# GpSimd's subtractions and additions issued as two operations of half the columns, in an attention and two-MLP kernel

## The chip, the core and the metric

The kernel runs on one core of a Trainium2 chip. Its engines work side by side, each on an instruction stream of its own: TensorE (PE in the profile; PEld is its weight loads), VectorE (DVE), ScalarE (ACT), GpSimd (POOL) and SyncE (SP), which issues most DMAs. The metric is the device time of the one core in microseconds.

## What is computed

The reference is three blocks, one after the other, on 4 batches of 576 tokens, d_model 512 (8 heads of 64):

```python
scores = scale * np.matmul(q, k.transpose(0, 1, 3, 2))
mask = (rel >= 0) & (rel < 128)
scores = np.where(mask, scores + bias[None], -1000000000.0)     # ALiBi bias, causal window of 128
attn = np.exp(scores - np.max(scores, axis=-1, keepdims=True))
attn = attn / (np.sum(attn, axis=-1, keepdims=True) + 1e-09)
x = heads_joined(np.matmul(attn, v))
# block 1
h = np.maximum(x.transpose(0, 2, 1) @ w_tok1, 0.0) @ w_tok2     # over tokens, 576 -> 256 -> 576
u = x + h.transpose(0, 2, 1)
u = u + np.maximum(u @ w_ch1, 0.0) @ w_ch2                      # over channels, 512 -> 1536 -> 512
# block 2
xn = (u - mean) / np.sqrt(var + 1e-06) * g_ln
out = u + np.maximum(xn @ w_ch1, 0.0) @ w_ch2                   # 512 -> 2048 -> 512
```

## The kernel before

The 2304 tokens are 18 tiles of 128. Every fp32 operand of a matmul is split into a high part and a low part: ScalarE rounds `x` to `hi` (fp32r), then `lo = x - hi` is made by VectorE or GpSimd. A product is then three matmuls (hi by hi, hi by lo, lo by hi), of 128x128 weights and 512 columns as a rule.

Three stages follow each other. **Attention with the token MLP** fills the first 150 us or so: per tile, scores (`ps_s`, L596), softmax on DVE and ACT, transposes (`ps_t`), masks by GpSimd (`pf`, L663), values (`ps_v`), and, a tile at a time, the token MLP (`tok`); GpSimd makes `xl = u - xh` of each tile and the low parts `wt1l`, `fewl` of its weights. **The channel MLP of block 1** and **that of block 2** follow. Each walks over tiles 0 to 7, then 16 and 17, then 8 to 15, and over the hidden features in steps of 256. The groups of eight tiles use a Strassen-like scheme with seven products (`seven_products`, L977): sums and differences of the input quarters (`st`, made by `prep_wide` from transposes `p`) and of the weight halves (`st`, made by `w1_of`, L930). Their low parts are `xl` and `w1l`; `w2l` is the low part of the second weight matrix. The hidden activations are `hh` (ACT) and `hl` (DVE). The second matmul of the MLP (`second`, L1036) writes `acc`, a PSUM tile with two buffers, and DVE adds each `acc` to the residual `u` (L1056); so PE can begin the `acc` after next only when DVE has done that addition.

Weights come as float64 and are decoded: `rh` and `rw` are loaded, ACT makes `e`, DVE makes `s` (L419, L421), `m` (L423) and `y` or `w` (L431). In block 2, `y` is scaled by g_ln (L476).

The order of instructions on every engine is computed while the program is built, by a list scheduler (`Plan.order`, L205). Each operation lists its cost on every engine that may take it; an operation that both DVE and POOL may take goes to POOL unless DVE would finish it sooner by the table (`sooner`, L223; DVE must win by 1200 ns). The costs are `dve(n)` = 150 + n/0.97 and `pool_tt(n)` = 150 + 2.4 n, in ns. The helper `minus` (L372) makes all the subtractions and additions above, and is called through `split` (L377), `split_x`, `w_split`, `x_tile`, `load_f64_split` and directly by `prep_wide` and `w1_of`; in the profile they all stand at line 374, told apart by their tiles. An engine takes its instructions strictly in the order of its stream.

Of the kernel before, what the change touches and what calls it, by code (L numbers as in the profile page):

```python
# [102 lines left out]
class Plan:  # L103
# [186 lines left out]
    def emit(self):  # L290
        for k in self.order():
            self.ops[k][1](self.taken[k])


def dve(n, fast=False):
    return 150 + n / (1.92 if fast else 0.97)
# [6 lines left out]
def pool_tt(n):  # L303
    return 150 + 2.4 * n
# [10 lines left out]
def block_kernel(tc, qT, kT, v, wt1, wt2, wa1, wa2, wb1, wb2, g, bias, out):  # L315
    nc = tc.nc
    NF1, NF2 = FF1 // P, FF2 // P
    pl = Plan()
# [5 lines left out]
    ENGINE = {"DVE": nc.vector, "POOL": nc.gpsimd}  # L324
# [30 lines left out]
    def several(x):  # L355
        return x if isinstance(x, list) else [x]
# [13 lines left out]
        pl.op({e: cost[e] for e in on}, emit, several(src), several(dst))  # L370

    def minus(dst, get, a, ga, b, gb, n, on=("DVE", "POOL"), alu=ALU.subtract, also=()):  # L372
        cost = {"DVE": dve(n), "POOL": pool_tt(n)}
        pl.op({e: cost[e] for e in on}, lambda e: ENGINE[e].tensor_tensor(get(), ga(), gb(), alu),  # L374
              [*several(a), *several(b), *also], several(dst))

    def split(hi, ghi, lo, glo, x, gx, n, on_hi=("ACT", "DVE", "POOL"), on_lo=("DVE", "POOL")):  # L377
        copy(hi, ghi, x, gx, n, on_hi)
        minus(lo, glo, x, gx, hi, lambda: ghi().bitcast(F32), n, on_lo)
# [287 lines left out]
    def normalize(i):  # L667

        rs = rs_t[i]
        ut = buf("atb", [P, H // 2, P], F32, "ut", 2)  # L670
        copy(ut, lambda: ut.t, pv, lambda: pv.t, DM, ("ACT",), True)

        def transposes():
            for p in range(4):
                nc.tensor.transpose(pv.t[:, p], ut.t[:, p], ident.t)

        op({"PE": 400}, transposes, [ut, ident], [pv])
        rc = buf("small", [P, H, 1], F32, "rc", 2)
        op({"POOL": 250}, lambda: nc.gpsimd.tensor_scalar(rc.t, rs.t, 1e-9, None, ALU.add), [rs], [rc])
        op({"DVE": 170}, lambda: nc.vector.reciprocal(rc.t, rc.t), [], [rc])  # L680
        minus(u[i], lambda: u[i].t.rearrange("p (h d) -> p h d", h=H), pv,
              lambda: pv.t.rearrange("p a (b d) -> p (a b) d", b=2), rc, lambda: rc.t.to_broadcast([P, H, D]), DM,
              ("DVE",), ALU.mult)
# [169 lines left out]
    def split_x(x, b, psum):  # L853

        hi, lo = x
        copy(hi, lambda: hi.t, b, lambda: b.t, CW, ("ACT",), psum)
        minus(lo, lambda: lo.t, b, lambda: b.t, hi, lambda: hi.t.bitcast(F32), CW, ("DVE",) if psum else ("DVE", "POOL"))
# [265 lines left out]
    for s in range(len(steps) + 1):  # L1123
# [5 lines left out]
        layer, c, tiles, n = steps[s]  # L1129
# [86 lines left out]
```

## Time and profile before

| | us |
|---|---|
| median of 3 runs | 854.21 (851.65 to 856.25) |
| the profiled execution | 853.47 |
| its span, first to last instruction | 851.8 |
| PE busy in it | 831.5 (98%) |
| DVE busy | 635.6 (75%) |
| ACT busy | 394.5 (46%) |
| POOL busy | 341.3 (40%) |

The profiled execution lies 0.74 us under the median and 1.7 us over its own span. A stretch of time in the profile is read by its busy time per engine, the clock that TensorE was granted (1.00 is its upper level, 2.4 GHz) and the list of waits; "idle 1.32 <-DVE u" behind an instruction says that its engine stood still for 1.32 us before it and that DVE's writing of `u` ended that.

### The profile page before, as it was taken

The page shows a single profiled execution, that of the slowest core. Times are in us where ns is not written, and L with a number is a line of the kernel's source. Part 1 is how long each engine was busy: PE and PEld are TensorE (multiplying, and loading weights), DVE is VectorE, ACT ScalarE, POOL GpSimd, SP SyncE. Part 2 cuts the span into 40 slices and gives each one's busy share as a digit, 9 for nine tenths or more (in the row PEclk, how much of TensorE's full clock was granted, in tenths as well). Part 3 has the DMA queues.
Part 4 walks back from the last instruction along what each step waited for, and adds up shares of the span by engine and source line. Part 5 has one row for each costly group of instructions (what it writes and reads, how often), then busy time and mean ns, then how long its engine had stood idle before and what let it go on. Part 6 is the DMA issues. An engine that isn't in the chain of part 4 may idle for free.

```text
span 851.8 us, 13204 instructions
## 1 busy us (share of the span) xinstructions
PE 831.5 (98%) x4478; PEld 687.5 (81%) x4478; DVE 635.6 (75%) x1308; ACT 394.5 (46%) x952; POOL 341.3 (40%) x356
## 2 busy tenths in 40 slices
PE   7999999989999999999998999999999999999998
PEld 6777878768888887788887888788889888888886
DVE  5787778987887989987888856988667755555554
ACT  6788776553434535234367322336358322222221
POOL 2675445554433656522236524614234712221110
PEclk9999999999999999999999999999999999999999
DMA  8678726467666799977752521777477762221112
GB/s 296 188 213 258 246 101 202 157 188 256 223 216 230 242 324 326 358 249 267 257 201 74 171 92 48 262 265 251 172 247 238 251 203 75 75 74 50 50 50 99
DMA packets 73698, 164.96 MB, mean 194 GB/s; under 512 B 8352, under 2 KB 8480, under 8 KB 73632
## 3 DMA queue, kind: packets, MB, share of 16 engines
q1 hardware_dynamic: 73152, 162.83, 56.6%
q0 software_dynamic: 480, 1.31, 0.7%
q8 instruction: 35, 0.57, 0.3%
q14 instruction: 31, 0.25, 0.1%
HBM read 131.34 MB, written 31.46 MB: 191 GB/s over the span
## 4 chain that ended last, share of the span: by engine, by line
PE 85%; DVE 7%; ACT 4%; DMA 1%; issue 1%; POOL 1%; SPq 0%; ACTq 0%; DVEq 0%; POOLq 0%
PE acc L1051 12%; PE acc L1052 12%; PE acc L1053 12%; PE b L993 10%; PE b L994 10%; PE b L995 10%; PE ps_v L608 3%; PE ps_s L596 3%; PE p L848 1%; PE b L442 1%; PE b L441 1%; PE b L440 1%; PE ps_t L653 1%; DVE st L374 1%; PE tok L735 1%
## 5 line engine op out<-in xcount | busy, mean ns | idle before, releaser
L1056 DVE TENSOR_TENSOR u<-acc,u 128x512 f32<-128x512 f32 x252 | 173.1, 687 | 67.6 <-PE acc L1053 64.8
L1051 PE MATMUL acc<-w2h,hh 128*128 128x512 f32 x504 | 198.6, 394 | 4.7 <-DVE u L1056 4.7
L1053 PE MATMUL acc<-w2h,hl 128*128 128x512 f32 x504 | 197.1, 391 | 0.2 <-DVE hl L926 0.2
L1052 PE MATMUL acc<-w2l,hh 128*128 128x512 f32 x504 | 197.1, 391 | 0.0
L924 ACT ACTIVATE hh<-b 128x512 fp32r<-128x512 f32 (+1 forms) x140 | 74.7, 553 | 260.4 <-PE b L995 225.5
L994 PE MATMUL b<-xl,w1h 128*128 128x512 f32 x392 | 153.2, 391 | 1.8 <-DVE xl L374 1.8
L993 PE MATMUL b<-xh,w1h 128*128 128x512 f32 x392 | 153.8, 392 | 1.2 <-DVE hl L926 0.9
L995 PE MATMUL b<-xh,w1l 128*128 128x512 f32 x392 | 153.4, 391 | 0.1
L926 DVE SCALAR_TENSOR_TENSOR hl<-b,hh 128x512 fp32r<-128x512 f32 (+1 forms) x140 | 85.8, 631 | 59.3 <-ACT hh L924 58.3
L374 POOL TENSOR_TENSOR w1l<-w,w1h 128x512 fp32r<-128x512 f32 (+1 forms) x56 | 70.9, 1266 | 127.5 <-ACT w1h L361 120.0
L1051 PEld LDWEIGHTS acc<-w2h,hh 128*128 128x128 f32 x504 | 95.0, 188 | 26.2 <-DVE u L1056 7.3
L1053 PEld LDWEIGHTS acc<-w2h,hl 128*128 128x128 f32 x504 | 95.0, 188 | 20.7 <-DVE hl L926 0.6
L1052 PEld LDWEIGHTS acc<-w2l,hh 128*128 128x128 f32 x504 | 95.0, 189 | 18.6
L374 POOL TENSOR_TENSOR w1l<-st,w1h 128x512 fp32r<-128x512 f32 x36 | 48.1, 1336 | 112.8 <-ACT w1h L361 105.5
L993 PEld LDWEIGHTS b<-xh,w1h 128*128 128x128 f32 x392 | 74.1, 189 | 17.4 <-DVE hl L926 1.3
L994 PEld LDWEIGHTS b<-xl,w1h 128*128 128x128 f32 x392 | 73.9, 189 | 17.4 <-DVE xl L374 2.3
L995 PEld LDWEIGHTS b<-xh,w1l 128*128 128x128 f32 x392 | 74.0, 189 | 16.0 <-DVE w1l L374 0.6
L416 ACT ACTIVATE e<-rh 128x512 bf16<-128x512 bf16 (+2 forms) x65 | 41.2, 634 | 71.7 <-DMA rh<-wb 38.1
L646 ACT ACTIVATE pr<-t,mn 128x128 f32<-128x128 f32 x144 | 55.9, 391 | 15.5 <-DVE mn L637 15.3
L663 POOL TENSOR_SCALAR_AFFINE_SELECT pf<-pf 128x512 f32<-128x512 f32 x64 | 42.3, 661 | 37.6 <-ACT pf L361 35.4
L374 DVE TENSOR_TENSOR b<-b,p 128x512 f32<-128x512 f32 x56 | 39.0, 697 | 22.2 <-PE b L995 21.7
L374 POOL TENSOR_TENSOR w2l<-w,w2h 128x512 fp32r<-128x512 f32 x23 | 32.3, 1405 | 48.0 <-ACT w2h L361 36.2
(118 smaller groups left out, 1368.2 us busy)
## 6 DMA issues: line engine op xcount, KB each, us to landing
w<-d SPq DMA_DIRECT2D x88, 256.0 KB, 4.3
rw<-wb SPq DMA_DIRECT2D x32, 512.0 KB, 4.9
rh<-wb SPq DMA_DIRECT2D x32, 512.0 KB, 4.9
rw<-wa SPq DMA_DIRECT2D x24, 512.0 KB, 4.0
rh<-wa SPq DMA_DIRECT2D x24, 512.0 KB, 4.4
d<-y SPq DMA_DIRECT2D x32, 256.0 KB, 4.3
keys<-kT SPq DMA_DIRECT2D x18, 256.0 KB, 3.8
q<-qT SPq DMA_DIRECT2D x18, 256.0 KB, 4.6
```

Of the source, the lines that this page charges most:

```text
L374: pl.op({e: cost[e] for e in on}, lambda e: ENGINE[e].tensor_tensor(get(), ga(), gb(), alu), [*several(a), *several(b), *also], several(dst))
L646: op({"ACT": 580}, lambda m=m: nc.scalar.activation(out=pr.t[:, m], in_=t.t[:, m], func=AF.Exp, bias=mn.t[:, m:m + 1], scale=-1.0, accum_o ...
L663: op({"POOL": 630}, lambda a=a: nc.gpsimd.affine_select(pf.t[:, a], pf.t[:, 1], [[0, 4], [1 - 2 * a, P]], (ALU.is_ge, ALU.is_gt)[a], 0.0, ...
L924: op({"ACT": act(n, True)}, lambda: nc.scalar.activation(out=hh.t[:, c], in_=go(), func=AF.Relu), [o], [(hh, key)])
L926: mark[0] = op({"DVE": dve(n)}, lambda: nc.vector.scalar_tensor_tensor(out=hl.t[:, c], in0=go(), scalar=0.0, in1=hh.t[:, c].bitcast(F32), ...
L993: nc.tensor.matmul(g.t, wh.t[:, w], xh.t, start=start and k == 0, stop=False, skip_group_check=True)
L994: nc.tensor.matmul(g.t, wh.t[:, w], xl.t, start=False, stop=False, skip_group_check=True)
L995: nc.tensor.matmul(g.t, wl.t[:, w], xh.t, start=False, stop=stop and k == 1, skip_group_check=True)
L1051: nc.tensor.matmul(o.t, hh.t[:, c:c + P], wh.t, start=j == 0, stop=False)
L1052: nc.tensor.matmul(o.t, hh.t[:, c:c + P], wl.t, start=False, stop=False)
L1053: nc.tensor.matmul(o.t, hl.t[:, c:c + P], wh.t, start=False, stop=j == 1)
L1056: op({"DVE": dve(DM)}, lambda o=o, i=i: nc.vector.tensor_tensor(u[i].t, o.t, u[i].t, ALU.add), [o], [u[i]])
```

## The change

`minus` issues its operation on GpSimd as two operations on the two halves of the columns, one behind the other, in the place of one; on VectorE it stays one operation. Its cost on POOL in the scheduler's table becomes twice the cost of a half.

```diff
     def minus(dst, get, a, ga, b, gb, n, on=("DVE", "POOL"), alu=ALU.subtract, also=()):
-        cost = {"DVE": dve(n), "POOL": pool_tt(n)}
-        pl.op({e: cost[e] for e in on}, lambda e: ENGINE[e].tensor_tensor(get(), ga(), gb(), alu),
-              [*several(a), *several(b), *also], several(dst))
+        cost = {"DVE": dve(n), "POOL": 2 * pool_tt(n // 2)}
+
+        def emit(e):
+            if e == "DVE":
+                return ENGINE[e].tensor_tensor(get(), ga(), gb(), alu)
+            for c in (slice(0, n // 2), slice(n // 2, n)):
+                ENGINE[e].tensor_tensor(get()[:, c], ga()[:, c], gb()[:, c], alu)
+
+        pl.op({e: cost[e] for e in on}, emit, [*several(a), *several(b), *also], several(dst))
```

For 512 columns the table's cost on POOL goes from 1379 to 1529 ns, for 256 columns from 764 to 914 ns. Since the table feeds the scheduler, the order changes on all engines. Counted in the two programs: GpSimd's 238 single operations of `minus` (147 of 512 columns, 4 of 288, 87 of 256) become 231 pairs of halves; no wait stands between the halves of a pair; a net 11 operations of `minus` go to VectorE, and one scaling by g_ln with them. All other operations keep their number. PE's stream is the same up to the second quarter of the attention, and differs later by where transposes and some groups of products stand.

Lines in the programs are those of each program (L374 before is L377 on DVE and L379 on POOL after; L1056 is L1062). Numbers in names count tiles as they are made, so `u_2150` before and `u_2178` after are the same tile of u.

VectorE, at the change from attention to the channel MLP: the last rows ahead of the low part `xl` (`xl_2500` before, `xl_2532` after) for which PE stands still in the profile. Before:

```order
L374 TENSOR_TENSOR st<-p_2409,st 128x512 x2
L419 TENSOR_SCALAR s<-e 128x256
L740 TENSOR_TENSOR u_2028<-tok,u_2028 128x512
L421 SCALAR_TENSOR_TENSOR s<-e,s 128x256
L740 TENSOR_TENSOR u_2150<-tok,u_2150 128x512
L374 TENSOR_TENSOR st<-p_2461,st 128x512
L374 TENSOR_TENSOR st<-w 128x256
L740 TENSOR_TENSOR u_2252<-tok,u_2252 128x512
L374 TENSOR_TENSOR st<-st,w 128x256
L374 TENSOR_TENSOR xl_2500<-p_2461,xh_2473 128x512
```

After:

```order
L746 TENSOR_TENSOR u_1915<-tok,u_1915 128x512
L377 TENSOR_TENSOR xl_2482<-st,xh_2457 128x512
L377 TENSOR_TENSOR st<-p_2381,st 128x512
L377 TENSOR_TENSOR st<-w 128x256
L746 TENSOR_TENSOR u_2050<-tok,u_2050 128x512
L377 TENSOR_TENSOR st<-st,w 128x256
L746 TENSOR_TENSOR u_2178<-tok,u_2178 128x512
L377 TENSOR_TENSOR st<-w,st 128x256
L425 TENSOR_SCALAR s<-e 128x256
L377 TENSOR_TENSOR xl_2532<-p_2381,xh_2427 128x512
```

From the pair `hl<-tok,hh` to this `xl` 18 operations stood on VectorE before, and 16 stand there now; a `w2l` and two additions to `u` are among those that went, and two operations of 256 columns and one `xl` are among those that came. PE's stream between the two has 55 rows before and 46 now.

VectorE, late in block 1 where tiles 16 and 17 end and tiles 8 to 15 begin, from one addition to `u` to the next for which PE stands still. Before:

```order
L1056 TENSOR_TENSOR u_2252<-acc,u_2252 128x512
L421 SCALAR_TENSOR_TENSOR s<-e,s 128x256
L926 SCALAR_TENSOR_TENSOR hl<-b_4138,hh 128x256
L374 TENSOR_TENSOR st<-p_4206,st 128x512 x2
L926 SCALAR_TENSOR_TENSOR hl<-b_4199,hh 128x256
L374 TENSOR_TENSOR st<-p_4233,st 128x512
L374 TENSOR_TENSOR xl_4269<-st,xh_4250 128x512
L374 TENSOR_TENSOR st<-st,w 128x256
L1056 TENSOR_TENSOR u_2150<-acc,u_2150 128x512
```

After:

```order
L1062 TENSOR_TENSOR u_2278<-acc,u_2278 128x512
L377 TENSOR_TENSOR st<-p_4353,st 128x512
L377 TENSOR_TENSOR st<-w 128x256
L377 TENSOR_TENSOR xl_4381<-p_4353,xh_4361 128x512
L377 TENSOR_TENSOR st<-st,w 128x256
L377 TENSOR_TENSOR xl_4396<-st,xh_4377 128x512
L377 TENSOR_TENSOR st<-st,w 128x256
L1062 TENSOR_TENSOR u_2178<-acc,u_2178 128x512
```

Nine operations between the two additions have become six. PE's stream has here three `acc` in a row before (18 matmuls), and now two `acc`, 18 matmuls of products, and two more `acc`.

VectorE, in block 2 where its tiles are prepared, around the addition for which PE stands still longest. Before:

```order
L1056 TENSOR_TENSOR u_1284<-acc,u_1284 128x512
L374 TENSOR_TENSOR st<-p_5693,st 128x512
L374 TENSOR_TENSOR st<-w 128x256
L374 TENSOR_TENSOR st<-st,w 128x256
L1056 TENSOR_TENSOR u_1416<-acc,u_1416 128x512
L374 TENSOR_TENSOR st<-w,st 128x256
L1056 TENSOR_TENSOR u_1517<-acc,u_1517 128x512
```

After:

```order
L1062 TENSOR_TENSOR u_1299<-acc,u_1299 128x512
L377 TENSOR_TENSOR st<-p_5826,st 128x512
L377 TENSOR_TENSOR st<-w 128x256
L1062 TENSOR_TENSOR u_1432<-acc,u_1432 128x512
L377 TENSOR_TENSOR st<-st,w 128x256
L1062 TENSOR_TENSOR u_1533<-acc,u_1533 128x512
L377 TENSOR_TENSOR st<-w,st 128x256
```

The operation `st<-st,w` has moved behind the addition to `u` that it preceded.

## Rows read from the trace of the kernel before

**Rows 1.** The page's part 1: busy us, share of the span, count.

```profile
PE 831.5 (98%) x4478; PEld 687.5 (81%) x4478; DVE 635.6 (75%) x1308; ACT 394.5 (46%) x952; POOL 341.3 (40%) x356
```

**Rows 2.** Busy time by stretches: us, each engine's busy us (count), PEclk, DMA share, GB/s.

```profile
150.00:182.00 32.00, 27.95 (x129) 21.94 (x128) 31.47 (x46) 18.64 (x34) 20.03 (x16) 0.95 0.43 144
182.00:325.00 143.00, 142.71 (x707) 120.39 (x706) 118.50 (x210) 61.39 (x117) 62.01 (x52) 1.00 0.74 253
325.00:333.00 8.00, 6.68 (x36) 5.42 (x35) 8.00 (x13) 5.14 (x10) 3.76 (x4) 1.00 0.98 334
333.00:460.00 127.00, 126.14 (x569) 103.35 (x567) 108.79 (x188) 58.88 (x121) 49.52 (x45) 1.00 0.71 246
460.00:470.00 10.00, 8.07 (x29) 6.17 (x28) 8.09 (x13) 4.13 (x8) 8.49 (x9) 0.83 0.30 105
470.00:533.00 63.00, 63.00 (x280) 52.18 (x279) 44.92 (x81) 20.67 (x40) 25.78 (x26) 1.00 0.32 107
533.00:540.00 7.00, 6.19 (x28) 4.80 (x27) 7.00 (x10) 2.90 (x5) 4.26 (x3) 1.00 0.68 214
```

**Rows 3.** Waits of PE: line, for whom, us in total, times, longest.

```profile
PE acc L1051 <- DVE u L1056: 4.7, 5, 1.9
PE b L994 <- DVE xl L374: 1.8, 1, 1.8
PE tok L735 <- DVE hl L713: 1.2, 1, 1.2
PE b L993 <- DVE hl L926: 0.9, 1, 0.9
```

**Rows 4.** Groups by shape on DVE: busy us, mean ns of one, idle before.

```profile
L926 DVE SCALAR_TENSOR_TENSOR hl<-b,hh 128x512 fp32r<-128x512 f32 x112 | 74.4, 685 | 55.3 <-ACT hh L924 54.6
L374 DVE TENSOR_TENSOR w1l<-st,w1h 128x512 fp32r<-128x512 f32 x20 | 20.0, 998 | 0.1
```

**Rows 5.** Timeline, 327 to 332 us: start, us, engine, line, operation.

```profile
327.96 2.99 POOL L374 TENSOR_TENSOR xl<-st,xh 128x512 fp32r<-128x512 f32 x2 [0.45 <-ACT xh L361]
328.07 1.74 DVE L374 TENSOR_TENSOR xl<-st,xh 128x512 fp32r<-128x512 f32 x1
...
329.73 1.50 DVE L374 TENSOR_TENSOR st<-st,w 128x256 f32<-128x256 f32 x1
...
331.75 0.41 DVE L374 TENSOR_TENSOR st<-w,st 128x256 f32<-128x256 f32 x1
331.89 0.50 PE L1051 MATMUL acc<-w2h,hh 128*128 128x512 f32 x1 [1.32 <-DVE u L1056]
```

**Rows 6.** Timeline, 175 to 179 us, POOL and DVE.

```profile
175.68 1.75 POOL L374 TENSOR_TENSOR w1l<-st,w1h 128x512 fp32r<-128x512 f32 x1 [0.30 <-ACT w1h L361]
...
176.19 1.79 DVE L431 SCALAR_TENSOR_TENSOR y<-m,s 128x512 f32<-128x512 uint32 x1
...
177.39 1.17 POOL L374 TENSOR_TENSOR st<-st,w 128x256 f32<-128x256 f32 x1
...
177.90 0.95 DVE L374 TENSOR_TENSOR w1l<-w,w1h 128x256 fp32r<-128x256 f32 x1
```

**Rows 7.** Timeline of DVE, two operations at the change of stages.

```profile
163.51 1.77 DVE L374 TENSOR_TENSOR xl<-st,xh 128x512 fp32r<-128x512 f32 x1
...
172.65 1.20 DVE L374 TENSOR_TENSOR st<-st,w 128x256 f32<-128x256 f32 x1
```

**Rows 8.** Timeline of DVE ahead of PE's longest wait in block 2.

```profile
462.64 0.80 DVE L374 TENSOR_TENSOR st<-w 128x256 f32<-128x256 f32 x1
463.37 0.94 DVE L374 TENSOR_TENSOR st<-st,w 128x256 f32<-128x256 f32 x1
```

**Rows 9.** Timeline of POOL in the attention, two operations back to back.

```profile
37.94 0.73 POOL L374 TENSOR_TENSOR wt1l<-y,wt1h 128x256 fp32r<-128x256 f32 x1
38.62 1.28 POOL L374 TENSOR_TENSOR xl<-u,xh 128x512 fp32r<-128x512 f32 x1
```

## The prediction

> **What bounds the kernel now.** I read the waits of PE first, then the busy time by stretches, then the timelines at the places where PE stood still. TensorE is busy for nearly the whole span, so the change can only act on what PE loses. After 150 us the stretches [rows 2] give that loss as length less PE busy: 4.05 us in 150 to 182, 0.29 to 325, 1.32 to 333, 0.86 to 460, 1.93 to 470, none to 533, 0.81 to 540, together 9.3. PE's waits [rows 3] name the cause: of these, 4.7 + 1.8 + 1.2 + 0.9 = 8.6 us are waits for VectorE, for an addition to `u` that gives an `acc` buffer back or for a low part. VectorE is busy for 75% on average [rows 1], but where PE waits it has nothing to spare: 31.47 of 32, 8.00 of 8 and 7.00 of 7 us [rows 2]. A second loss is the clock. It was granted at 0.95 over 150 to 182 and 0.83 over 460 to 470 [rows 2], so it fell from the upper to the lower of its levels for part of them, behind PE's two longest waits (1.8 and 1.9 us); behind the 1.32 us wait at 331 it stayed at 1.00. The work lost is 0.05 x 32 = 1.6 and 0.17 x 10 = 1.7 us. So some 12.6 us after 150 us are within reach.
>
> **Why VectorE is late there.** At 331.89 PE waited 1.32 us for `u`. VectorE's two operations just ahead took 1.74 and 1.50 us [rows 5]. One of 512 columns that reads PSUM takes 0.685 [rows 4] and one of 256 with two inputs in SBUF that ran while POOL was idle took 0.41 [rows 5]. So 1.06 and 1.09 us were lost, and in that time GpSimd ran two `xl` of 512 columns, 327.96 to 330.95 [rows 5]. Each VectorE operation ended a little after a GpSimd operation did. The same holds for `w1l`, which takes 0.998 us on average over 20 [rows 4] against 0.685. A VectorE operation with two inputs in SBUF therefore waits for the GpSimd operation in progress to end, however far that has to go. That wait is what the change cuts.
>
> **Part 1: the halves.** Does the VectorE operation get in between two GpSimd operations that stand back to back? At 176.19 VectorE's `y` met the `w1l` that ran to 177.43. The next GpSimd operation began at 177.39 with no idle before it, yet `y` ended at 177.98, and it was that second one that took 1.17 in place of 0.73 [rows 6, 9]. So it does get in, one operation at a time. Behind a whole operation the loss is up to 1.09 [rows 5]; behind one of 256 columns, the size of a new half, it was 0.95 - 0.41 = 0.54 [rows 6] and 0.80 - 0.41 = 0.39, 0.94 - 0.41 = 0.53 [rows 8]. I take half of every loss behind a 512-column operation as gone. GpSimd pays with a second fixed cost. An operation of 512 columns takes 1.28 and one of 256 takes 0.73 [rows 9], so a pair costs 2 x 0.73 - 1.28 = 0.18 more. For 128 columns there is no row: the line through the two gives 0.46 and again 0.18 a pair; it can't exceed 0.73 (a pair then costs 0.73 more) and hardly be under 0.37 (nothing more). With 231 pairs GpSimd gets 231 x 0.18 = 42 us busier, from 341 [rows 1] to some 380, under half of the span.
>
> The Trainium skill (SBUF — State Buffer, Who interferes with whom) says that GpSimd and a VectorE instruction with two SBUF inputs share a port pair that is held as an exclusive lock for the whole instruction, and that the other blocks fully; by that, too, the loss is set by the length of GpSimd's instruction, and rows 5 and 6 agree.
>
> **Part 2: the places, one by one.** *At 331* the losses of 1.06 and 1.09 become about 1.08 together; the wait of 1.32 would shrink to 0.24, and the new order eases it besides (six operations between the two additions instead of nine, and PE does 18 product matmuls before it needs that buffer). Gain 1.1. *At 464* the wait is 1.93. The operation `st<-st,w` of 0.94 now stands behind the addition [rows 8], though its start-to-start cost was 0.87, and half of the other's 0.39 goes: 1.93 - 0.87 - 0.2 = 0.86, gain 1.1. I take 1.0, since a `w2l` moved to VectorE stands 0.6 us of work earlier there. *At 538* the order is unchanged and the wait 0.81 stands behind a VectorE that is full; its operations there are stalled alike, gain 0.8 at most, and I take it. *At the change of stages*, three waits: the one for `hl` (1.2) gains little, as one more operation of VectorE stands ahead of it (I take 0.4). The one for `xl` (1.8) loses half of 1.77 - 0.685 and of 1.20 - 0.41 [rows 7], that is 0.94; VectorE has 1.2 us less to do between the two (18 operations to 16; ten of 512 columns at 0.60 from start to start instead of twelve, the rest small); but PE has nine rows less to do meanwhile, one matmul and eight short transposes: at 63.00/280 = 0.225 us a matmul [rows 2] 2.0 at most, and I take 1.2. Net 0.9. The one for `hl` in block 1 (0.9) loses half of `y`'s 1.79 - 0.685 [rows 4, 6], 0.55, and I take 0.5. Gain 1.8. *The small waits* in 182 to 325 and 333 to 460, 1.15 together: half, 0.6. The sum is 1.1 + 1.0 + 0.8 + 1.8 + 0.6 = 5.3 us.
>
> **Part 3: the clock.** If the two longest waits fall under the 1.32 us behind which the clock stayed up, its 1.6 + 1.7 = 3.3 us come back too. By the sums above they fall to about 0.8 and 0.9. I take both, and neither for the far end.
>
> **Part 4: what it costs.** In the attention GpSimd stands in a chain of mask, `wt1l`, `xl`, PE's `tok` [rows 9], where its lateness can reach PE. There are 27 pairs there (18 `xl`, 5 `wt1l`, 4 `fewl`); 27 x 0.18 = 4.9 us at most. Most tiles have ACT and PE work beside it, so I take 1.0. After it, 12 operations come to VectorE, about 12 x 0.6 = 7 us, mostly where it has 14 to 29% free (108.79 of 127, 44.92 of 63) [rows 2]; the new order will also put some waits where none were, which nothing in the trace before can show. I take 2.0 for these, between 0 and the 5.3 that Part 2 gains.
>
> **The sum** is 5.3 + 3.3 - 1.0 - 2.0 = 5.6 us. Against the profiled execution's 853.5 that is 847.9; the runs' median lies 0.7 higher, so I say **848.6** for the median after.
>
> **The rivals.** *The waits form again elsewhere.* VectorE's saving is real but the scheduler's new order and 7 us more VectorE work bring back what Part 2 gains, and one long wait still drops the clock: 848.6 plus half of Part 2 (2.7) and one clock (1.7) is 853, between 850 and 854. For it: PE's waits lie at a handful of places of 0.8 to 1.9 us [rows 3], and any reshuffle can make such a place. Against it: the three places that I followed lose operations ahead of the waits.
>
> *The halves act as one.* If GpSimd's second half takes its turn ahead of a waiting VectorE operation, VectorE waits for 1.4 instead of 1.28 and the change doesn't do what it is written to do: nothing of Part 2 comes, 1.0 of Part 4 does, and waits grow by a tenth: 855.5 to 856. Against it: rows 6, where the second of two back-to-back operations was the one that waited. The skill's page says that whichever starts first gets the lock; the second half is queued early, so by that rule alone either could win. By that rule the time would be this rival's; rows 6 are against it.
>
> *GpSimd becomes late (slower than before).* The place is the attention's chain of mask, low part and `tok`. All 27 pairs at 0.18 there are 4.9 us, and VectorE's relief doesn't help since ACT and GpSimd set the pace: with Part 2's gains cancelled that gives 859. It decides from the point where GpSimd's pairs cost over 0.4 us each, or all 0.18 reach PE, and the later stages give back under 3 us. Against it: GpSimd is not full even where it is used most before 460 us, 20.03 of 32 [rows 2].
>
> **How the numbers follow.** Forecast 0.53 (844 to 850), waits form again 0.25 (850 to 854), halves as one 0.10 (855 to 857), late GpSimd 0.12 (857 to 861). What counts as a difference here is 0.5%, 4.3 us, about what a measurement of this kernel can tell from no change: faster is under 849.9. The forecast's own spread has its upper end there. So faster 0.53, same 0.35, slower 0.12. The range goes from 843.5 (all of Part 2's and Part 3's gains with little of the cost, 853.5 - 10, which also lies within the 12.6 us in reach) to 857.
>
> **What would show it.** Right: VectorE busy falls from 636 by 20 us or more although it does 12 more operations; `w1l<-st` of 512 columns on VectorE falls from 0.998 to some 0.84; POOL's busy time rises by 25 to 45 us; the waits at 331, 464 and 538 are under 1 us; and the granted clock stays at 1.00 in block 2. Wrong: VectorE operations still take 1.5 to 1.8 us; new waits of PE on POOL in the first 150 us; a new wait over 1.3 us with a fall of the clock behind it.

## The result, and the profile after

| | before | after |
|---|---|---|
| median, us | 853.44 of 5 runs (851.65 to 856.25) | 843.70 of 5 runs (842.30 to 844.09) |
| ratio, 95% interval | | 0.9882 (0.9867 to 0.9897) |
| the profiled execution, its span | 853.47, 851.8 | 843.42, 841.7 |

The change makes the kernel 9.7 us faster, 1.2%. The forecast had the direction and about half of the size: its sum was 5.6 us, and its 848.6 lies 4.8 us under the 853.44 of before measured beside it. Part 1 of the page of after, which answers to [rows 1]:

```profile
PE 825.9 (98%) x4478; PEld 684.3 (81%) x4478; DVE 624.9 (74%) x1320; ACT 394.7 (47%) x952; POOL 373.1 (44%) x575
```

VectorE's busy time fell by 10.7 us though it does 12 operations more, GpSimd's rose by 31.8, and PE's fell by 5.6 with the same 4478 matmuls, mostly since less of its time runs at the lower clock. (GpSimd's single operations of `minus` before are 242, not the 238 of the section on the change: 91 of them have 256 columns. Less the 11 that moved, that gives the 231 pairs.) PE's waits after, in full, to be held against [rows 3] (engine, what waited, for which engine's what: us in total, times, longest):

```profile
PE ps_v L681 <- ACT ut L361: 2.2, 3, 1.2
PE ps_s L602 <- DMA q<-qT: 1.5, 1, 1.5
PE tok L765 <- POOL ident masks.py:199: 1.4, 1, 1.4
PE ps_t L659 <- ACT pf L361: 1.4, 2, 0.7
PE b L1001 <- POOL w1l L379: 1.2, 2, 0.8
PE ps_v L614 <- DMA v<-v: 0.9, 1, 0.9
PE acc L1057 <- DVE u L1062: 0.8, 1, 0.8
PE tok L447 <- POOL xl L379: 0.8, 2, 0.4
PE b L1000 <- DVE xl L377: 0.4, 1, 0.4
PE acc L1059 <- DVE hl L932: 0.2, 1, 0.2
```

The 4.7 us for `u`, 1.8 for `xl`, and 1.2 and 0.9 for `hl` of before have become 0.8 for `u`, 0.4 for `xl` and 0.2 for `hl`; new are 1.2 us for GpSimd's `w1l`, and 0.8 for its `xl` in the attention, where before waits twice 0.1. The 0.8 for `u` is no new wait. It is what is left of the 1.93 at 464: PE's stream around it is the same, and the same addition to `u` ends it. The second trace of before that is used below, then after:

```profile
463.39 0.50 PE L1051 MATMUL acc<-w2h,hh 128*128 128x512 f32 x1 [1.93 <-DVE u L1056]
457.47 0.50 PE L1057 MATMUL acc<-w2h,hh 128*128 128x512 f32 x1 [0.79 <-DVE u L1062]
```

After comes to this place 6 us earlier. So the short stretches of [rows 2] no longer hold the same work, and longer ones are compared.

**Where the time came from.** Executions differ at their start. In the first 25 us the granted clock is 0.93 in the first trace of before and 1.00 in a second one, whose span is 850.2; in after's trace it is 1.00, but PE waits 2.4 us for the loads of `q` and `v` up to 72 us, waits which two later runs with after's order (320 and 192 columns, below) don't have. So stretches are compared from 139.5 us on, with the second trace of before, whose waits from there on are those of [rows 3] within 0.2 us. That trace by longer stretches (window, its length, busy us and count of PE, PEld, DVE, ACT, POOL, then granted clock, DMA share and GB/s):

```profile
139.50:188.00 48.50, 44.37 (x237) 35.68 (x236) 44.92 (x69) 26.62 (x49) 26.35 (x23) 0.96 0.55 178
295.00:356.00 61.00, 59.04 (x318) 50.15 (x318) 56.35 (x107) 25.07 (x48) 34.35 (x31) 1.00 0.97 335
437.00:496.00 59.00, 56.60 (x250) 45.68 (x249) 49.68 (x90) 30.19 (x61) 29.41 (x28) 0.97 0.35 116
496.00:578.00 82.00, 81.18 (x358) 66.89 (x357) 62.86 (x100) 27.13 (x53) 32.85 (x31) 1.00 0.57 183
```

And after:

```profile
139.50:188.00 48.50, 47.58 (x268) 38.50 (x263) 42.68 (x72) 29.50 (x54) 37.75 (x52) 1.00 0.65 208
295.00:356.00 61.00, 60.06 (x324) 51.45 (x323) 54.48 (x107) 25.60 (x49) 40.95 (x59) 1.00 0.96 327
437.00:496.00 59.00, 57.99 (x265) 47.39 (x264) 45.05 (x85) 30.17 (x63) 31.26 (x49) 1.00 0.32 99
496.00:578.00 82.00, 82.00 (x363) 67.85 (x362) 64.44 (x107) 30.82 (x60) 42.84 (x64) 1.00 0.60 198
```

Length less PE's busy time went from 4.13, 1.96, 2.40 and 0.82 us to 0.92, 0.94, 1.01 and 0: gains of 3.2, 1.0, 1.4 and 0.8, together 6.4. The clock falls twice in this trace of before, behind the waits of 1.84 and 1.93 us. Over the ten microseconds that hold each fall (172 to 182 and 460 to 470) it is 0.83, so each costs 0.17 x 10 = 1.7 us, and both, 3.4 us, come back. That is 9.8 us behind the attention.

The spans of these two traces differ by 850.2 - 841.7 = 8.5 us. The rest lies ahead: at the last wait for `ut` (`ps_v`), at 77.11 us before and 78.85 after, after is 1.7 us late, 0.6 of it by the two waits for GpSimd's `xl`, most of the rest by the waits for `q` and `v`, which are this execution's. 9.8 - 1.7 = 8.1 of the 8.5 us are thus accounted for. Without those loads it would be 9.2, to be held against the 9.7 between the medians.

### The profile page after: what moved, and what is told of

Its sections match the earlier page's. It is cut to its first block, busy times and chain, and to the rows that moved or that the text cites. A ratio compares the mean times of both kernels' runs of the same rounds, so it can differ in the third digit from the quotient of the medians.

```text
span 841.7 us, 13438 instructions
## 1 busy us (share of the span) xinstructions
PE 825.9 (98%) x4478; PEld 684.3 (81%) x4478; DVE 624.9 (74%) x1320; ACT 394.7 (47%) x952; POOL 373.1 (44%) x575
## 4 chain that ended last, share of the span: by engine, by line
PE 88%; POOL 3%; DMA 3%; ACT 2%; issue 2%; DVE 1%; SPq 0%; POOLq 0%; ACTq 0%; DVEq 0%
PE acc L1057 13%; PE acc L1059 13%; PE acc L1058 13%; PE b L1001 10%; PE b L999 10%; PE b L1000 10%; PE ps_v L614 3%; PE ps_s L602 2%; PE p L854 2%; PE b L448 1%; PE b L447 1%; PE b L446 1%; DMA v<-v 1%; PE ps_t L659 1%; PE tok L447 1%
## 5 line engine op out<-in xcount | busy, mean ns | idle before, releaser
L1062 DVE TENSOR_TENSOR u<-acc,u 128x512 f32<-128x512 f32 x252 | 173.1, 687 | 69.1 <-PE acc L1059 66.1
L379 POOL TENSOR_TENSOR w1l<-w,w1h 128x256 fp32r<-128x256 f32 (+1 forms) x96 | 70.6, 758 | 141.8 <-ACT w1h L361 137.6
L379 POOL TENSOR_TENSOR w1l<-st,w1h 128x256 fp32r<-128x256 f32 x74 | 58.1, 808 | 99.2 <-ACT w1h L361 93.3
L377 DVE TENSOR_TENSOR b<-b,p 128x512 f32<-128x512 f32 x56 | 39.0, 696 | 22.4 <-PE b L1001 21.7
L379 POOL TENSOR_TENSOR st<-w 128x128 f32<-128x128 f32 x76 | 40.1, 553 | 32.5 <-DMA w<-d 20.0
```

The lines of the kernel that those rows point to most:

```text
L379: ENGINE[e].tensor_tensor(get()[:, c], ga()[:, c], gb()[:, c], alu)
L1062: op({"DVE": dve(DM)}, lambda o=o, i=i: nc.vector.tensor_tensor(u[i].t, o.t, u[i].t, ALU.add), [o], [u[i]])
```

## Experiments

Two things change at once: how GpSimd issues, and, through the table of costs, the order on every engine. The theory: an operation of GpSimd in progress holds up VectorE, shorter ones hold it up for less, and PE's waits for VectorE shrink by that, twice over where they also cost the clock. The rivals: the new order alone does it; the halves bring nothing by themselves; GpSimd pays with lateness.

### The two parts of the change, one at a time

The order of after, GpSimd's operations whole:

```diff
         cost = {"DVE": dve(n), "POOL": 2 * pool_tt(n // 2)}
 
         def emit(e):
-            if e == "DVE":
-                return ENGINE[e].tensor_tensor(get(), ga(), gb(), alu)
-            for c in (slice(0, n // 2), slice(n // 2, n)):
-                ENGINE[e].tensor_tensor(get()[:, c], ga()[:, c], gb()[:, c], alu)
+            ENGINE[e].tensor_tensor(get(), ga(), gb(), alu)
```

> The cost table, and so the order on every engine, is that of the changed kernel; GpSimd issues each operation whole. Theory (shorter GpSimd operations, since VectorE waits for the one in progress): most of the gain is gone, 849 to 853 us, with VectorE operations again at 1.5 to 1.8 us beside GpSimd's of 512 columns; what stays is the work that the new order takes from ahead of the waits at the change of stages and at 464 us (2 us and perhaps one clock fall). Rival (the new order makes the gain): 843 to 846 us.

The halves, in the order of before:

```diff
-        cost = {"DVE": dve(n), "POOL": 2 * pool_tt(n // 2)}
+        cost = {"DVE": dve(n), "POOL": pool_tt(n)}
```

> The cost table and the order are those of the kernel before; GpSimd issues halves. Theory (shorter operations): 844 to 848 us; the wait of 1.32 at 331 us falls to 0.2 to 0.4, that at 538 us goes, both clock falls after 150 us go. Rival (the new order makes the gain): 851 to 854 us, the waits stay within 0.3 us of before. Halves that act as one: the stalls of VectorE are no shorter than before, 855 us.

Measured: the order alone 847.50 us, ratio 0.9937 (0.9920 to 0.9955); the halves alone 844.67, ratio 0.9906 (0.9889 to 0.9922). By the medians, against 853.28 of before on that chip, they bring 5.8 and 8.6 us, and together (after) 9.7. The two add up to 14.4, so their gains overlap. PE's two largest sums of waits for VectorE behind the attention, in the order alone:

```profile
PE acc L1054 <- DVE u L1059: 1.7, 3, 0.8
PE b L997 <- DVE xl L376: 1.6, 1, 1.6
```

Four of its stretches:

```profile
139.50:188.00 48.50, 45.24 (x247) 36.31 (x246) 44.37 (x68) 27.89 (x51) 30.25 (x25) 1.00 0.57 189
295.00:356.00 61.00, 59.35 (x322) 50.91 (x321) 56.87 (x107) 25.55 (x49) 34.02 (x30) 1.00 0.93 323
437.00:496.00 59.00, 57.83 (x262) 46.84 (x261) 48.59 (x87) 28.94 (x59) 27.36 (x25) 1.00 0.32 105
496.00:578.00 82.00, 81.21 (x359) 66.88 (x357) 66.03 (x104) 30.01 (x57) 36.43 (x33) 1.00 0.57 189
```

The halves alone, PE's three largest sums of waits for VectorE:

```profile
PE b L999 <- DVE hl L932: 2.0, 1, 2.0
PE acc L1057 <- DVE u L1062: 1.4, 1, 1.4
PE b L1000 <- DVE xl L377: 1.1, 1, 1.1
```

And the same four stretches:

```profile
139.50:188.00 48.50, 44.71 (x237) 35.79 (x236) 43.18 (x70) 26.93 (x49) 32.40 (x42) 0.96 0.56 186
295.00:356.00 61.00, 60.89 (x330) 52.40 (x329) 55.72 (x112) 25.37 (x49) 42.40 (x61) 1.00 0.97 346
437.00:496.00 59.00, 57.39 (x262) 46.91 (x262) 47.60 (x87) 28.91 (x59) 33.44 (x53) 1.00 0.35 121
496.00:578.00 82.00, 82.00 (x363) 67.92 (x362) 62.00 (x104) 31.20 (x60) 44.05 (x63) 1.00 0.57 191
```

What each takes away can be read place by place. The wait at 538 goes with the halves (82.00 busy of 82) and stays with the order alone (81.21), where that order is the same as before. In 295 to 356 the halves alone leave 0.11 us of 1.96, the order alone 1.65: the wait for `u` at 331 goes there too, but two others take its place (0.7 for GpSimd's `w1l`, 0.9 for `b`). At 464 the wait falls from 1.93 to 1.39 with the halves and to 0.68 with the order, and the clock stays at 1.00 with either. At the change of stages neither takes all: the order alone leaves a wait of 1.6 for `xl` (at full clock), the halves alone one of 2.0 for `hl`, behind which the clock falls again (0.96) in this trace. Only both together come down to 0.92 us idle. The trace of the halves alone is that of its longest execution, 846.60 us at a mean granted clock of 0.998; the other three took 844.32 to 844.90 at 1.000, so by these numbers they don't have that fall. The halves by themselves are thus real, here worth more than the order, and so is the order.

At one order, the page's part 1 tells what the halves do to the engines. The order alone:

```profile
PE 826.8 (98%) x4478; PEld 684.0 (81%) x4478; DVE 640.7 (76%) x1320; ACT 394.7 (47%) x952; POOL 328.3 (39%) x344
```

Against it, after has VectorE busy for 15.8 us less, with the same 1320 operations, and GpSimd for 44.8 us more over 231 pairs, 0.19 a pair, its own waiting for VectorE included (Part 1 of the prediction had 0.18). By groups the 15.8 us lie in the decode of the weights: `m` falls from 37.8 to 30.9 us, the two groups of `s` from 33.3 to 28.3 and 23.9 to 20.1, `y` from 33.3 to 30.4, while `w` rises from 13.4 to 14.4, 17.6 in all. VectorE's subtractions and additions gain nothing in sum: `st<-st,w`, for one, falls from 689 to 534 ns on average, and `w1l<-st` rises (below). `m<-rw` and `s<-e` (the second of those two) have one input, so "two inputs in SBUF" in the prediction is too narrow. The new order itself costs VectorE 640.7 - 635.3 = 5.4 us (635.3 in the second trace of before).

### How much of it is the order's luck

The same whole operations with other additions to the table, 75 and 300 ns (after adds 150):

```diff
-        cost = {"DVE": dve(n), "POOL": pool_tt(n)}
+        cost = {"DVE": dve(n), "POOL": pool_tt(n) + 75}
```

(`+ 300` in the second of them.)

> Whole GpSimd operations; the table's cost of minus on GpSimd is 75 ns higher than before, half of what the changed kernel adds, so that the scheduler makes another order again. If the order of the changed kernel was lucky, this one lies at 851 to 856 us; if moving some operations from GpSimd to VectorE is what the order gains by, it lies between the kernel before and the run with only the order changed, 848 to 851 us.

> As the last, with 300 ns more, twice what the changed kernel adds. Moving operations is what gains: 845 to 848 us, since still more go to VectorE. An order by luck: anywhere between 846 and 858 us, with no relation to the 75 and 150 ns.

And the kernel before itself, timed and profiled once more:

> The kernel before, once more, for a second trace. If the fall of the clock in the first 25 us (0.93 there before, 1.00 in the changed kernel) belongs to one execution and not to the kernel, it is absent here, PE reaches the scores of the fourth tile about 1.2 us earlier, and the mean clock of its runs differs between 0.994 and 0.997 or so. If it belongs to the order of the kernel before, it is here again and in every run. The waits at 173, 331, 464 and 538 us come again within 0.2 us in either case.

Measured: 846.41 us, ratio 0.9933 (0.9918 to 0.9948), with 75; 854.00, ratio 1.0016 (1.0006 to 1.0026), with 300; the kernel before 852.58, ratio 1.0001 (0.9989 to 1.0012). So an order bought with 75 or 150 ns brings 6 us, and one bought with 300 loses one: the gain does not follow from how much work moves to VectorE. Each of the four orders has its waits at other places; with 300, one of PE's waits, at the change of stages, makes up for all that went elsewhere:

```profile
PE b L994 <- DVE xl L374: 4.1, 1, 4.1
```

### Without the attention's pairs, and without the narrow ones

25 of GpSimd's 27 halved operations of the attention (`xl` of 16 tiles, `wt1l`, `fewl`) made whole again, by a new argument `parts` of `minus`; the `xl` of the last two tiles stay halved. In part:

```diff
-        split(hi, ghi, lo, glo, *load_f64(src, k, n), n, ("ACT",), ("POOL",))
+        split(hi, ghi, lo, glo, *load_f64(src, k, n), n, ("ACT",), ("POOL",), 1)
...
-              ("POOL",) if i < NTILE - 2 else ("DVE", "POOL"))
+              ("POOL",) if i < NTILE - 2 else ("DVE", "POOL"), 1 if i < NTILE - 2 else 2)
```

> As the changed kernel, but the 27 operations of the attention stage on GpSimd (xl of a tile, wt1l, fewl) stay whole, with their old cost in the table; halves everywhere else. Theory: the two waits of PE of 0.39 us for xl at 39 and 53 us go back to 0.10, some 0.6 us in all, 842.5 to 843.7 us, the rest unchanged. Rival (halves help in the attention too): 844 to 846 us.

And then the operations of 256 and 288 columns too, in the same order:

```diff
-            for c in (slice(k * n // parts, (k + 1) * n // parts) for k in range(parts)):
+            m = parts if n == DM else 1
+            for c in (slice(k * n // m, (k + 1) * n // m) for k in range(m)):
```

> The order of the kernel with the attention's operations whole; GpSimd issues halves of the 512-column operations alone, and the 256-column ones (st, some w1l) whole. Theory: a 256-column operation delays VectorE by at most 0.54 us and its halves cost GpSimd 0.18 more, so nothing is lost and GpSimd's w1l comes earlier where PE waits for it (1.2 us at 329): 841.5 to 842.7 us. Rival (every halving helps): 843.5 to 845 us.

Measured: 842.66 us, ratio 0.9879 (0.9865 to 0.9894), and 844.14, ratio 0.9905 (0.9888 to 0.9921). In the trace of the first the two waits for the attention's `xl` fall from 0.39 to 0.10 each, 0.6 us in all where Part 4 charged 1.0, and the rest is nearly as in after (the waits for `w1l` are 1.6 in place of 1.2). But the two ratios, 0.9882 and 0.9879, are not told apart by their intervals. Halving only the 512-column operations leaves PE idle for 0.76, 1.00, 1.52 and 0.28 us in the four stretches, 3.6 in all, against 3.1 of `attention_whole`: the narrow pairs are worth about half a microsecond, which the totals don't resolve either. (That trace is of an execution of 842.06 us, 2.1 under the median.)

The order of 75 ns, with halves behind the attention:

```diff
-        cost = {"DVE": dve(n), "POOL": parts * pool_tt(n // parts)}
+        cost = {"DVE": dve(n), "POOL": pool_tt(n) + 75}
```

> The order of the run with whole operations at 75 ns more (846.4 us), with GpSimd issuing halves everywhere but in the attention stage. If the gains of halves and order add at the places where PE still waits there (538 us 0.81, the w1l at 330 us 1.2, two small waits for hl at 457 and 581 us), 842 to 843.5 us. If they overlap as in the changed kernel, which lies 3.8 us under its own order with whole operations, 842.6 us is the floor and the two kernels are the same. Rival: GpSimd becomes late with halves in this order too, 845 to 848 us.

Measured 842.29 us, ratio 0.9878 (0.9863 to 0.9892): at a second order the halves, here behind the attention only, bring 846.41 - 842.29 = 4.1 us, less than at the old one (8.6) and about as much as at after's (847.50 - 843.70 = 3.8). It is the shortest median seen, but its interval and after's overlap almost wholly.

### Four parts

If shorter is better, quarters should be better still, until GpSimd's added cost makes it late.

```diff
-            for c in (slice(0, n // 2), slice(n // 2, n)):
+            for c in (slice(k * n // 4, (k + 1) * n // 4) for k in range(4)):
```

> The order of the changed kernel, each GpSimd operation of minus issued as four quarters. Theory: VectorE's stalls shrink once more, by less than half, but PE has only 1.4 us of waits for VectorE left, and GpSimd's operations grow by another 0.35 us each, which PE meets at the four places where it now waits for GpSimd (2.0 us there): 843 to 847 us. Rival (the length of the operation is all that counts): under 842.5 us.

And with the attention's operations whole, in the order of `attention_whole`:

```diff
-            for c in (slice(k * n // parts, (k + 1) * n // parts) for k in range(parts)):
+            m = 2 * parts if parts > 1 else 1
+            for c in (slice(k * n // m, (k + 1) * n // m) for k in range(m)):
```

> The order of the kernel with the attention's operations whole, GpSimd issuing quarters in the place of halves after that stage. With quarters everywhere the loss against halves was 8.8 us: 2.9 us up to 139 us, 3.6 at the change of stages, 2.5 near 331 us, 2.2 near 464. Theory (GpSimd is late there with w1l): only the attention's share goes, 847 to 850 us, with waits of 2 to 3 us for w1l. Rival (the attention's lateness pushed the rest): 842.5 to 845 us.

Measured: 852.51 us, ratio 1.0007 (0.9990 to 1.0024); with the attention's operations whole 850.21, ratio 0.9975 (0.9952 to 0.9997). VectorE is freer than ever, 610.5 us busy in the first of them, and all of the gain is lost; in the second all but 3 us of it. Part 1 of the page of the quarters (an execution of 855.49 us):

```profile
PE 831.8 (97%) x4478; PEld 687.7 (81%) x4478; DVE 610.5 (72%) x1320; ACT 394.4 (46%) x952; POOL 456.9 (54%) x1037
```

PE's waits for GpSimd's `w1l` in them:

```profile
PE b L1001 <- POOL w1l L379: 5.4, 3, 3.1
```

Two `w1l` in GpSimd's timeline at the change of stages (start, us, engine, line, operation):

```profile
176.69 4.04 POOL L379 TENSOR_TENSOR w1l<-st,w1h 128x128 fp32r<-128x128 f32 x8
```

And there in after:

```profile
171.70 3.37 POOL L379 TENSOR_TENSOR w1l<-st,w1h 128x256 fp32r<-128x256 f32 x4
```

They take 4.04 us in quarters and 3.37 in halves, and they begin 5 us later. PE waits 5.4 us for `w1l`, 3.1 of it at once, and behind that the clock falls, to 0.93 over 175 to 200; it falls again behind the next, of 2.06 us at 339. This is the prediction's third rival, late GpSimd. It is real, only not at two parts, and its main places are these two and not the attention, since keeping the attention whole gives back but 2.3 us.

### Where in GpSimd's operation VectorE arrives

One row spoke against the theory: `w1l<-st` of 512 columns on VectorE, which was to fall from 0.998 us to 0.84. VectorE's groups by form (count, busy us, mean ns, idle before) in the order alone:

```profile
L426 DVE TENSOR_SCALAR m<-rw 128x512 uint32<-128x512 uint32 x56 | 37.8, 675 | 0.3
L376 DVE TENSOR_TENSOR w1l<-st,w1h 128x512 fp32r<-128x512 f32 x19 | 18.4, 967 | 0.1
```

And in after:

```profile
L429 DVE TENSOR_SCALAR m<-rw 128x512 uint32<-128x512 uint32 x56 | 30.9, 553 | 0.3
L377 DVE TENSOR_TENSOR w1l<-st,w1h 128x512 fp32r<-128x512 f32 x19 | 21.4, 1129 | 0.1
```

The decode `m<-rw` gained, 675 to 553 ns, but `w1l<-st` lost, 967 to 1129. In block 2 it meets a `w1l` of GpSimd again and again. One such meeting in the timeline of before (rows of ACT, DVE and POOL):

```profile
749.97 0.60 ACT L924 ACTIVATE hh<-b 128x512 fp32r<-128x512 f32 x1 [10.69 <-PE b L995]
750.46 0.62 ACT L361 ACTIVATE w1h<-w 128x512 fp32r<-128x512 f32 x1
750.60 0.69 DVE L926 SCALAR_TENSOR_TENSOR hl<-b,hh 128x512 fp32r<-128x512 f32 x1 [1.30 <-ACT hh L924]
...
751.16 1.30 POOL L374 TENSOR_TENSOR w1l<-w,w1h 128x512 fp32r<-128x512 f32 x1 [5.34 <-ACT w1h L361]
751.33 0.69 DVE L1056 TENSOR_TENSOR u<-acc,u 128x512 f32<-128x512 f32 x1
...
751.93 1.08 DVE L374 TENSOR_TENSOR w1l<-st,w1h 128x512 fp32r<-128x512 f32 x1
```

The two operations that meet, in after:

```profile
741.01 1.44 POOL L379 TENSOR_TENSOR w1l<-w,w1h 128x256 fp32r<-128x256 f32 x2 [5.05 <-ACT w1h L361]
741.78 1.22 DVE L377 TENSOR_TENSOR w1l<-st,w1h 128x512 fp32r<-128x512 f32 x1
```

VectorE comes 0.77 us behind GpSimd's start in both. Both are tied to ScalarE's stream: `hh` releases VectorE's `hl`, behind which stand an addition to `u` and the `w1l`, and the `w1h` right behind that `hh` releases GpSimd. At that moment 0.53 us of the whole operation was left. Of a pair, the first half (0.73) has just ended and the second has begun, with 0.67 left. If it is this fixed phase that counts and not a half of the length on average, an uneven cut must decide it (320 columns first, and 192 in place of 320 in a second run):

```diff
-            for c in (slice(0, n // 2), slice(n // 2, n)):
+            for c in (slice(0, n * 320 // 512), slice(n * 320 // 512, n)):
```

> The changed kernel's order with uneven parts: the first part of GpSimd's two has 320 of 512 columns (200 of 320 for any width), the second 192. In block 2 VectorE's `w1l<-st` begins 0.77 us after GpSimd's pair begins, time after time (741.78 against 741.01). Theory fixed phase: what such an operation loses is what is left of GpSimd's part at that moment, not half of a part's length on average. From 1.28 us for 512 columns and 0.73 for 256, 320 columns are estimated at 0.87 us, so only 0.10 us is left at 0.77: the 13 operations that now take 1.22 us take about 0.7, and the group's mean falls from 1.13 to under 0.85. Rival theory, any phase: the loss goes by the sum of the squares of the parts' lengths, 0.87 squared + 0.59 squared = 1.10 against 2 x 0.73 squared = 1.07, so the mean stays within 0.05 of 1.13. Both theories: PE does not wait for these operations in block 2, so the total stays at 842 to 846 us.

> The mirror image: the first part has 192 of 512 columns (estimated 0.59 us), the second 320 (0.87 us). Theory fixed phase: at 0.77 us after the pair's begin the second part has 0.59 + 0.87 - 0.77 = 0.69 us left, so the 13 operations of `w1l<-st` in block 2 stay at 1.2 to 1.25 us and the group's mean at 1.10 to 1.17. Rival theory, any phase: the same mean as with 320 columns first. The total stays at 842 to 846 us by either.

Measured: 843.12 us, ratio 0.9887 (0.9868 to 0.9906), and 843.64, ratio 0.9892 (0.9870 to 0.9914). VectorE's group with 320 columns first:

```profile
L377 DVE TENSOR_TENSOR w1l<-st,w1h 128x512 fp32r<-128x512 f32 x19 | 13.6, 715 | 0.1
```

The two operations that meet:

```profile
740.35 1.92 POOL L379 TENSOR_TENSOR w1l<-w,w1h 128x320 fp32r<-128x320 f32 x2 [5.17 <-ACT w1h L361]
741.12 0.68 DVE L377 TENSOR_TENSOR w1l<-st,w1h 128x512 fp32r<-128x512 f32 x1
```

The group with 192 first:

```profile
L377 DVE TENSOR_TENSOR w1l<-st,w1h 128x512 fp32r<-128x512 f32 x19 | 21.5, 1133 | 0.1
```

The two operations that meet:

```profile
741.35 1.44 POOL L379 TENSOR_TENSOR w1l<-w,w1h 128x192 fp32r<-128x192 f32 x2 [5.17 <-ACT w1h L361]
742.12 1.22 DVE L377 TENSOR_TENSOR w1l<-st,w1h 128x512 fp32r<-128x512 f32 x1
```

715 ns against 1133, with parts of the same two sizes. For these operations the phase decides, and any rule that averages over it falls. It also shows who waits otherwise: with 320 first VectorE takes 0.68 us and GpSimd's pair 1.92 in place of 1.44. The total does not move; PE doesn't wait for these operations.

## What the prediction had right, and what it mis-sized

**The mechanism held.** VectorE waits for the GpSimd operation in progress, and gets in between two that stand back to back: at the same order the halves made VectorE's 1320 operations 15.8 us shorter. The second rival, that the halves act as one, falls with it. What the Trainium skill (SBUF — State Buffer, SBUF: two separate sides) says of a port pair held for the whole instruction agrees with the meetings above, where the operation of either engine grows with what the other's has left: VectorE's by 0.39 us with 0.53 left, by 0.54 with 0.67 left.

**Part 1** had 0.18 us a pair and GpSimd at some 380; it was 0.19, and 373.1. Its other sentence, half of every loss gone, was wrong as a general rule. It gave VectorE a fall of 20 us net of some 7 us of moved work; 10.7 came net, and 15.8 at one order. Where VectorE's arrival is tied to GpSimd's start by the same producer, halving can save nothing or even cost 0.14 us an operation.

**The step that failed is Part 2's sum at the change of stages, with Part 4's 2.0 for new waits.** The mechanism was right there, and the sizes were not. PE's waits of the second trace of before, place by place, and what after has left of them, in us:

| term of the prediction | before | after | gained | forecast |
|---|---|---|---|---|
| at 331 | 1.32 | 0 | 1.32 | 1.1 |
| at 464 | 1.93 | 0.79 | 1.14 | 1.0 |
| at 538 | 0.82 | 0 | 0.82 | 0.8 |
| change of stages, three waits | 4.13 | 0.42 | 3.71 | 1.8 |
| small waits | 1.11 | 0.22 | 0.89 | 0.6 |
| Part 2 together | | | 7.9 | 5.3 |
| Part 3, the clock | | | 3.4 | 3.3 |
| Part 4, the attention | | | -0.6 | -1.0 |
| Part 4, new waits behind it | | 1.19 | -1.2 | -2.0 |
| sum | | | 9.5 | 5.6 |

The new waits are the two for GpSimd's `w1l`, of 0.37 and 0.82 us. By the stretches the gain behind the attention without the clock was 6.4; by this table it is 7.9 - 1.2 = 6.7, and the 0.3 between them is idle time in pieces too short for the list.

Of the 3.9 us that the forecast fell short of this sum, 1.9 lie at the change of stages. There the prediction let the token MLP's wait for `hl` gain 0.4, since the order burdens it: with the halves alone it falls from 1.2 to 0.3, with both it is gone. It let the one for `hl` in block 1 gain 0.5 from the halves: with the halves alone it is 2.0 in place of 1.1, and with the order alone it is gone, which the prediction had not followed there. The one for `xl` falls from 1.8 to 1.1 with the halves, to 1.6 with the order and to 0.4 with both, where 0.9 was forecast. So each of the three fell further, by the halves and the order together, than was worked out one by one. Another 0.8 is the 2.0 for new waits, for which no row stood: 1.2 came. The places that had been followed through order and halves, 331, 464 and 538, came out within 0.25 of the forecast.

**Part 3** was right: both falls of the clock went.

**The first rival** (waits form again, one drops the clock) did not come at this order; 300 ns in the table shows that it could have. **The third**, late GpSimd, came with quarters. What the sign rested on was less sure than the forecast's argument made it: more than half of what after gained is also to be had from its order alone, and no step of the prediction asked how much hangs on the 150 ns in the table. That 150 ns gave a good order is in part luck.

## What to carry to other kernels

Where two engines hold each other up by whole instructions, shorten those of the engine that has slack, and only until its own results come late: here two parts gained 0.5 to 1.0% at one and the same order, four gained nothing. What a shorter instruction saves the other engine depends on where in it that engine arrives, so look whether one producer releases both before taking an average. And when an edit also feeds a scheduler's table, time the table and the edit apart: here each alone brought over half of the gain, and together far less than their sum.

## What had not been expected of the hardware

- The clock stayed at 1.00 behind single waits of PE of 1.59 us (the order alone, ended at 173.65 us) and 1.72 us (halves in the order of 75 ns, ended at 328.26), and fell behind 1.84 and 1.93 (before) and 1.95 (the halves alone). The prediction had only dared 1.32. But the length of the last wait does not tell it all: in the first 25 us of the run with 75 ns the clock fell at 19 us, behind waits of 0.70 and 0.69, and it stayed at 1.00 in the order alone behind 1.45 and 0.69 at the same place.
- An operation of GpSimd on two inputs of 128 columns takes 0.46 us where nothing is in its way, as the line through 512 and 256 had it; so four of them cost 0.56 more than the one of 1.28. The attention's 18 `xl` of 512 columns average 1314 ns whole (the order alone), 770 a half (after) and 498 a quarter.
- The waiting goes both ways: where VectorE's `w1l` meets GpSimd's, an uneven cut of GpSimd's operation moves the whole loss from one engine to the other (1.22 and 1.44 us against 0.68 and 1.92).
- In the first 25 us the granted clock was 0.93 in some executions (one trace of before, the quarters, 75 ns) and 1.00 in others (the other trace of before, after, the rest); the two traces of before differ by 1.6 us of span.
